# Issuing v and the DMA transposes one step ahead in a fused attention and MLP kernel

## The chip, the cores and the metric

One core of one Trainium2 chip. Times are microseconds of device time for one execution. A "span" is what the profile covers, from the first to the last instruction of one execution; a run takes about 2 us more than its span. Ratios are the mean time of one kernel's fast runs over that of the kernel before in the same rounds, so not quite the ratio of the medians that are quoted beside them.

## The reference

Causal attention over 8 batches of 8 heads, 576 positions, 64 channels, with a bias from cumulative sums of `s`, and then a two-layer MLP on the 4608 tokens:

```python
s_pos = np.maximum(s, 0.0)
cum = np.cumsum(s_pos, axis=-1)
bias = -(cum[:, :, :, None] - cum[:, :, None, :])
scores = np.where(causal, -1000000000.0, scores + np.minimum(bias, 0.0))
attn = softmax(scores)                 # cut: written out in the reference
x = (attn @ v).transpose(0, 2, 1, 3).reshape(B * S, H * D)
h = x @ w_in                           # 512 -> 2048
out = gelu(h) @ w_out                  # 2048 -> 512
```

## The kernel before

The order of instructions on each engine is the order of the program. A step `c` of the main loop runs the MLP on 512 tokens (`l1_item` is the first layer, `l2_item` the second) and, in between, the attention of the next batch `nb = c + 1`. Heads go in four pairs. There are nine steps. The first seven carry a batch, and the last two are MLP only and are called the tail here. "Start" is what comes before the first layer of step 0.

The data of a batch comes in three ways. Casting DMAs (`cast_rows`, issued by GpSimd) copy q and k to bf16 in DRAM, transposing DMAs (`transpose_rows`, on the SP queue) bring them into `qkT`, and `load_v` (SP queue) brings v. The bias is folded into weights, so v is scaled by `wb` on VectorE (`scale_v`). GpSimd sums the squares of v, which feed a check that decides whether a slow general path must run (`square_v`). P are the exponentials of the scores, `xT` is the output of the attention and the input of the MLP, and `o_sb` is the copy of a second-layer result that is then stored. In the views PE is TensorE, PEld its weight loads, DVE VectorE, ACT ScalarE, POOL GpSimd and SPq the SP queue.

```python
for c in range(NCH):
    nb = c + 1
    l1_item(c, 0, 0, KO - 1)           # ... first layer, items 0 and 1
    if nb < B:
        scale_v(nb, STS, nc.vector)    # VectorE: five tensor_tensor of 128x512
    if nb + 1 < B:
        cast_rows(nb + 1)              # GpSimd queue: 8 casting DMAs
    for f2 in range(2, FT // 2):
        l1_item(c, f2)
    if nb < B:
        exp_set()
        l2_item(c, 0, 0, 4)
        sc_item(nb, 0)                 # scores, exp on ACT, masks on VectorE
        l2_item(c, 0, 4)
        absmax(nb, 0)
        square_v(nb)                   # GpSimd: ten tensor_tensor of 128x512 f32
        for p in range(1, NP):
            sc_item(nb, p)
            av_item(nb, p - 1)         # 28 output matmuls; needs P masked, v scaled
            l2_item(c, p, 0, 12)
            absmax(nb, p)
            # ...
        if nb + 1 < B:
            transpose_rows(nb + 1)     # SP queue: 8 transposing DMAs
            load_v(nb + 1, [nc.sync])  # SP queue: 5 loads, behind them
```

Of the kernel before, what the change touches and what calls it, by code (L numbers as in the profile page):

```python
# [19 lines left out]
def kernel(  # L20
# [10 lines left out]
    nc = tc.nc  # L31
    fp32 = mybir.dt.float32
    bf16 = mybir.dt.bfloat16
# [5 lines left out]
    B, H, S, D = q.shape  # L39
    scale = 1.0 / (D ** 0.5)  # L40
    BH = B * H
    ST = 5
    NR = 6
    PR = S // NR
    SL = S - 512
    NP = H // 2
# [17 lines left out]
    PW = sum(UW)  # L64
# [51 lines left out]
    w_in_r = const.tile([128, KO, dff], bf16, name="w_in_r")  # L116
    w_out_r = const.tile([128, FT, KO * 128], bf16, name="w_out_r")
    vv = [const.tile([128, ST, H, D], bf16, name=f"vv{i}") for i in range(2)]
    qk_bf = const.tile([PR, 2, NR, H, D], bf16, name="qk_bf")
    qkT = [const.tile([128, 2, NP, 640], bf16, name=f"qkT{i}") for i in range(2)]  # L120
    for t in vv:
        nc.gpsimd.memset(t[64:128, ST - 1, :, :], 0.0)
# [8 lines left out]
    def load_qk(n, p):  # L131
        src = q if n == "q" else k
        if p == 0:
            raws[0, n] = work.tile([PR, H, NR, D], fp32, tag=f"raw{n}", bufs=1, name=f"raw_{n}")
        nc.sync.dma_start(
            out=raws[0, n][:, 2 * p : 2 * p + 2].rearrange("p h r d -> p h (r d)"),
            in_=bass.AP(
                tensor=src.tensor,
                offset=src.offset + 2 * p * S * D,
                ap=[[NR * D, PR], [S * D, 2], [1, NR * D]],  # L140
            ),
        )

    def cast(n, p, eng):
        hs = slice(2 * p, 2 * p + 2)
        i = 0 if n == "q" else 1
        eng.tensor_copy(
            qk_bf[:, i, :, hs].rearrange("p r h d -> p h r d"), raws[0, n][:, hs]
        )
# [55 lines left out]
    def scale_v(b, sts, eng, h0=0, h1=H):  # L205
        t = raws[b, "v"]
        vb = vv[b % 2]
        for st0, st1 in sts:
            n_st = 128 if st1 < ST else SL
            eng.tensor_tensor(  # L210
                vb[:n_st, st0:st1, h0:h1, :],
                t[:n_st, st0:st1, h0:h1, :],
                wb[:n_st, st0:st1, b * H + h0 : b * H + h1]
                .unsqueeze(3).to_broadcast([n_st, st1 - st0, h1 - h0, D]),
                op=MULT,
            )
# [3 lines left out]
    def load_w(which, i):  # L220
        if which == 0:
            src = moe_w_in.rearrange("(ko p) f -> p ko f", p=128)[:, :, i * 512 : (i + 1) * 512]
            dst = w_in_r[:, :, i * 512 : (i + 1) * 512]
        else:
            src = moe_w_out.rearrange("(fo p) m -> p fo m", p=128)[:, i * 4 : (i + 1) * 4, :]
            dst = w_out_r[:, i * 4 : (i + 1) * 4, :]
        nc.gpsimd.dma_start(out=dst, in_=src)
# [12 lines left out]
    def weights_pe():  # L240
        t_ps = ps.tile([128, ST, BH], fp32, tag="av", bufs=3, name="t_ps")
        for st in range(ST):
            n_st = 128 if st < ST - 1 else SL
            nc.tensor.transpose(
                t_ps[:n_st, st, :], cum[:, st * 128 : st * 128 + n_st], ident[:64, :64]
            )
        nc.scalar.activation(wb[:, 0 : ST - 1], t_ps[:, 0 : ST - 1], func=AF.Exp)
        nc.scalar.activation(wb[:SL, ST - 1], t_ps[:SL, ST - 1], func=AF.Exp)
# [97 lines left out]
    P_of = {}  # L346

    def sc_item(b, p):
        P_of[b, p] = P = work.tile([128, 2, PW], bf16, tag="P", bufs=2, name="P")
        for u in range(NU):  # L350
            s_ps = ps.tile([128, 2, 512], fp32, tag="sc", bufs=2, name="sc_ps")
            for jt, i0, n, off in UNITS[u]:
                for e in range(2):
                    nc.tensor.matmul(  # L354
                        s_ps[:, e, off : off + n],
                        lhsT=qkT[b % 2][e * 64 : e * 64 + 64, 1, p, jt * 128 : jt * 128 + 128],
                        rhs=qkT[b % 2][e * 64 : e * 64 + 64, 0, p, i0 : i0 + n],
                        start=True, stop=True,
                    )
            nc.scalar.activation(  # L360
                P[:, :, UO[u] : UO[u] + UW[u]], s_ps[:, :, : UW[u]], func=AF.Exp, scale=scale
            )
            d = P[:, :, UO[u] : UO[u] + 512].rearrange("p e (g c) -> p e g c", c=256)[:, :, :, 0:128]
            nc.vector.tensor_tensor(  # L364
                d, d, tri_bf.unsqueeze(1).unsqueeze(1).to_broadcast([128, 2, 2, 128]), op=MULT
            )
            if u == 1:
                d = P[:, :, UO[u] + 448 : UO[u] + 512]
                nc.vector.tensor_tensor(  # L369
                    d, d, tri_bf[:, :64].unsqueeze(1).to_broadcast([128, 2, 64]), op=MULT  # L370
                )

    def av_item(b, p):
        P = P_of[b, p]
        vb = vv[b % 2]
        todo = []
        for c, (c0, cn) in enumerate(ICH):
            o_ps = ps.tile([128, 2, 256], fp32, tag="av", bufs=3, name="av")
            for den in range(2):
                for n_part, (jt, lo, n, off) in enumerate(PARTS[c]):  # L380
                    for e in range(2):
                        nc.tensor.matmul(  # L382
                            o_ps[e * 64 : e * 64 + 64, den, lo : lo + n],
                            lhsT=(
                                wb[:, jt, b * H + 2 * p + e : b * H + 2 * p + e + 1].to_broadcast([128, 64])
                                if den
                                else vb[:, jt, 2 * p + e, :]
                            ),
                            rhs=P[:, e, off : off + n],
                            start=(n_part == 0),  # L390
                            stop=n_part == len(PARTS[c]) - 1,
                            skip_group_check=True,
                        )
            todo.append(o_ps)
        for c, (c0, cn) in enumerate(ICH):
            o_ps = todo[c]
            ln = work.tile([128, 256], fp32, tag="ln", bufs=3, name="ln")
            nc.scalar.activation(ln[:, :cn], o_ps[:, 1, :cn], func=AF.Ln, scale=math.exp(-LNC[c]))  # L398
            nc.scalar.activation(  # L399
                ln[:, :cn], ln[:, :cn], func=AF.Exp, scale=-1.0, bias=lnb[:, c : c + 1]  # L400
            )
            t0 = b * S + c0
            nc.vector.tensor_tensor(xT[:, p, t0 : t0 + cn], o_ps[:, 0, :cn], ln[:, :cn], op=MULT)  # L403
# [54 lines left out]
    for p in range(NP):  # L458
        cast("q", p, nc.gpsimd)
        cast("k", p, nc.gpsimd)  # L460

    def start_pair(p):
        tr_item(p, 0)
        tr_item(p, 1)
        sc_item(0, p)

    ALLV = [(0, ST - 1), (ST - 1, ST)]
    start_pair(0)
    weights_pe()
    start_pair(1)  # L470
    scale_v(0, ALLV, nc.vector, 0, 2)
    av_item(0, 0)
    for i in range(4):
        load_w(0, i)
    scale_v(0, ALLV, nc.gpsimd, 4, 8)
    cast_rows(1)
    for i in range(4):
        load_w(1, i)
    transpose_rows(1)
    load_v(1, [nc.sync])  # L480
    square_v(0)
    start_pair(2)
    scale_v(0, ALLV, nc.vector, 2, 4)
    av_item(0, 1)
    start_pair(3)
    av_item(0, 2)
    av_item(0, 3)
    for p in range(NP):
        absmax(0, p)

    for c in range(NCH):
        nb = c + 1
        l1_item(c, 0, 0, KO - 1)
        l1_item(c, 1, 0, KO - 1)
        l1_item(c, 0, KO - 1)
        l1_item(c, 1, KO - 1)
        if nb < B:
            scale_v(nb, STS, nc.vector)
        if nb + 1 < B:
            cast_rows(nb + 1)  # L500
        for f2 in range(2, FT // 2):
            l1_item(c, f2)
        if nb < B:
            exp_set()
            l2_item(c, 0, 0, 4)
            sc_item(nb, 0)
            l2_item(c, 0, 4)
            absmax(nb, 0)
            square_v(nb)
            for p in range(1, NP):  # L510
                sc_item(nb, p)
                av_item(nb, p - 1)
                l2_item(c, p, 0, 12)
                absmax(nb, p)
                if p == NP - 1:
                    av_item(nb, p)
                l2_item(c, p, 12)
            if nb + 1 < B:
                transpose_rows(nb + 1)
                load_v(nb + 1, [nc.sync])  # L520
            if c == 0:
                cert_decay()
        else:
            for sub in range(4):
                l2_item(c, sub)
                if c == B - 1:
                    (cert_1, cert_2, cert_3, cert_4)[sub]()
# [150 lines left out]
```

## Time and profile before

The median is 425.02 us (four runs, 422.63 to 431.89), the span of the profiled run 420.4. I cut the span into steps at the first matmul of each first layer in the TensorE timeline:

| | start | step 0 | steps 1 to 5, mean | step 6 | tail |
|---|---|---|---|---|---|
| before | 39.1 | 49.2 | 43.8 | 43.7 | 69.3 |

The page of the profile: busy time of TensorE, and in 40 slices of 10.5 us the granted clock of TensorE in tenths.

```profile
PE 335.9 (80%) x2426; PEld 171.6 (41%) x2426; DVE 208.7 (50%) x353; ACT 224.2 (53%) x356; POOL 206.6 (49%) x169
...
PEclk9999995999889997999699989996999799999999
```

TensorE is 80% busy, and the clock falls to half again and again, once in most steps. The waits of TensorE (what it waited for, us in total, how often, the longest):

```profile
PE av L382 <- DVE P L364: 40.5, 14, 10.7
PE o_ps L437 <- DVE o_sb L444: 7.8, 15, 1.2
```

The great wait is that of the output matmuls (`av`) for VectorE's mask of P. One step shows it, in the TensorE timeline (start, us, what, how many; in brackets the idle time before and who ended it):

```profile
132.05 3.62 PE L420 MATMUL h_ps<-xT,w_in_r 128*128 128x512 bf16 x16
...
151.07 0.62 PE L354 MATMUL sc_ps<-qkT_101 64*128 64x256 bf16 x10
157.02 0.53 PE L382 MATMUL av<-P,vv_98 128*64 128x256 bf16 x4 [5.33 <-DVE P L364]
...
158.43 0.64 PE L382 MATMUL av<-P,vv_98 128*64 128x256 bf16 x6 [0.55 <-DVE P L364]
...
160.01 5.29 PE L437 MATMUL o_ps<-w_out_r,gT 128*128 128x512 bf16 x16 [0.23 <-DVE o_sb L444]
```

TensorE has nothing to do from 151.7 to 157.0. The timeline of VectorE says why the mask is late:

```profile
148.60 0.69 DVE L210 TENSOR_TENSOR vv_98<-raw_v,wb 128x512 bf16<-128x512 f32 x1 [14.80 <-DMA raw_v<-in_v_dram]
...
151.58 0.82 DVE L210 TENSOR_TENSOR vv_98<-raw_v,wb 128x512 bf16<-128x512 f32 x1 [0.85 <-DMA raw_v<-in_v_dram]
154.37 2.27 DVE L210 TENSOR_TENSOR vv_98<-raw_v,wb 128x512 bf16<-128x512 f32 x2 [1.96 <-DMA raw_v<-in_v_dram]
156.56 1.81 DVE L364 TENSOR_TENSOR P<-P,tri_bf 128x512 bf16<-128x512 bf16 x2
158.30 1.05 DVE L369 TENSOR_TENSOR P<-P,tri_bf 128x128 bf16<-128x128 bf16 x1
```

VectorE's queue is in order. The five scalings of v stand in front of the masks and wait for v, which arrives piece by piece from 148.6 us on, the fourth of five pieces at 154.4, so 16 to 22 us into the step that began at 132.05. v is late because of its place on the SP queue: eight transposes, 1.2 us of issue each, are ahead of it.

```profile
134.70 1.16 SPq L167 DMA_TRANSPOSE qkT_101<-rows_0_0_1025  x1
...
143.79 1.22 SPq L167 DMA_TRANSPOSE qkT_101<-rows_1_3_1039  x1
145.10 2.17 SPq L173 DMA_DIRECT2D raw_v<-in_v_dram  x3
```

After the idle time TensorE is slow. These are stretches of the same step, each with its length, the busy time of the engines (PE, PEld, DVE, ACT, POOL, each with the number of its instructions), the granted clock, the DMA share (it adds up the times of packets and goes above 1 in some views) and GB/s:

```profile
157.00:160.00 3.00, 2.20 (x28) 1.98 (x28) 3.00 (x4) 1.33 (x4) 2.92 (x3) 0.50 0.00 0
160.00:165.30 5.30, 5.29 (x18) 1.92 (x19) 5.30 (x8) 0.91 (x3) 5.22 (x6) 0.68 0.13 50
```

The clock is 0.50 for 3 us and 0.68 for the next 5. The Trainium skill ("TensorE: Matmul & The Clock Gate", What's actually happening) says that the clock gate halves TensorE's clock after an idle window of about 3.4 us, that the window runs freely, and that a busy one brings full speed back. The trace agrees with the halving: 0.50 after 5.3 us of idle time.

### The profile page before, as it was taken

How to read it: one execution, taken by the hardware profiler on the slowest of the kernel's cores; microseconds unless marked ns; L12 is line 12 of the kernel's file. 1: busy time of each engine (PE TensorE's matmuls, PEld its weight loads, DVE VectorE, ACT ScalarE, POOL GpSimd, SP SyncE). 2: the span in 40 equal slices, each digit the busy share in tenths (PEclk: the TensorE clock that was granted, in tenths of full speed). 3: DMA queues.
4: the chain of work that ended last, by engine and by line, in shares of the span. 5: the costliest groups of instructions: out<-in, count | busy, mean ns of one | idle time of the engine just before them, and what ended most of it. 6: DMA issues, size and time to landing. Idle time of an engine off the chain costs nothing.

```text
span 420.4 us, 6347 instructions
## 1 busy us (share of the span) xinstructions
PE 335.9 (80%) x2426; PEld 171.6 (41%) x2426; DVE 208.7 (50%) x353; ACT 224.2 (53%) x356; POOL 206.6 (49%) x169
## 2 busy tenths in 40 slices
PE   2447953999499949996899868995999599988983
PEld 1335422544345424543454335443544354433431
DVE  4446316760985059705971397229831984023011
ACT  1447662586548554856286727773667457501500
POOL 8889999900993089505980499039001920000000
PEclk9999995999889997999699989996999799999999
DMA  8999998966389454956097809880127201011011
GB/s 202 211 189 172 183 175 83 128 105 148 48 97 132 112 101 52 138 123 128 25 151 110 154 26 132 117 167 27 50 76 152 51 27 51 0 51 51 1 51 55
DMA packets 148150, 42.58 MB, mean 101 GB/s; under 512 B 137808, under 2 KB 143441, under 8 KB 148113
## 3 DMA queue, kind: packets, MB, share of 16 engines
q0 software_dynamic: 69632, 12.46, 37.1%
q1 hardware_dynamic: 78480, 29.65, 31.5%
q8 instruction: 21, 0.34, 0.3%
q14 instruction: 17, 0.13, 0.1%
HBM read 36.85 MB, written 17.69 MB: 130 GB/s over the span
## 4 chain that ended last, share of the span: by engine, by line
PE 48%; DVE 16%; DMA 14%; SPq 14%; issue 4%; ACT 2%; POOL 1%; DVEq 0%; ACTq 0%; POOLq 0%
PE o_ps L437 24%; PE h_ps L420 18%; DMA raw_v<-in_v_dram 11%; SPq L167 8%; SPq L173 5%; PE av L382 4%; DVE P L364 4%; DVE vv_97 L210 3%; DVE P L369 3%; DVE vv_98 L210 2%; DVE o_sb L444 2%; ACT gT L426 2%; DMA rows_1_0_278<-in_k_dram 2%; PE sc_ps L354 1%; DVE amx L184 1%
## 5 line engine op out<-in xcount | busy, mean ns | idle before, releaser
L437 PE MATMUL o_ps<-w_out_r,gT 128*128 128x512 bf16 x576 | 142.8, 400 | 8.4 <-DVE o_sb L444 7.8
L420 PE MATMUL h_ps<-xT,w_in_r 128*128 128x512 bf16 x576 | 127.2, 379 | 6.2 <-ACT gT L426 6.2
L194 POOL TENSOR_TENSOR sq<-raw_v 128x512 f32<-128x512 f32 (+1 forms) x40 | 57.4, 1435 | 124.0 <-DMA raw_v<-in_v_dram 124.0
L426 ACT ACTIVATE gT<-h_ps 128x1024 bf16<-128x1024 f32 x63 | 63.5, 1022 | 60.5 <-PE h_ps L420 60.5
L360 ACT ACTIVATE P<-sc_ps 128x1024 bf16<-128x1024 f32 x64 | 62.0, 1021 | 60.3 <-PE sc_ps L354 55.4
L437 PEld LDWEIGHTS <-gT 128*128 128x128 bf16 x576 | 56.7, 102 | 78.2 <-issue 23.1
L420 PEld LDWEIGHTS <-w_in_r 128*128 128x128 bf16 x576 | 56.2, 98 | 75.2 <-issue 8.7
L195 POOL TENSOR_TENSOR sumv<-sumv,sq 128x512 f32<-128x512 f32 (+1 forms) x40 | 57.2, 1430 | 3.1
L210 DVE TENSOR_TENSOR vv_98<-raw_v,wb 128x512 bf16<-128x512 f32 (+1 forms) x20 | 21.5, 1092 | 67.4 <-DMA raw_v<-in_v_dram 67.4
L398 ACT ACTIVATE ln<-av 128x256 f32<-128x256 f32 (+1 forms) x96 | 30.7, 320 | 43.2 <-PE av L382 42.9
L444 DVE COPY o_sb<-o_ps 128x512 f32<-128x512 f32 x36 | 24.5, 681 | 53.7 <-PE o_ps L437 53.6
L364 DVE TENSOR_TENSOR P<-P,tri_bf 128x512 bf16<-128x512 bf16 x64 | 41.1, 660 | 18.0 <-ACT P L360 17.8
L399 ACT ACTIVATE ln<-ln,lnb 128x256 f32<-128x256 f32 (+1 forms) x96 | 43.6, 454 | 3.1
L210 DVE TENSOR_TENSOR vv_97<-raw_v,wb 128x512 bf16<-128x512 f32 (+2 forms) x19 | 21.9, 1188 | 46.5 <-DMA raw_v<-in_v_dram 46.4
L403 DVE TENSOR_TENSOR xT<-av,ln 128x256 bf16<-128x256 f32 (+1 forms) x96 | 32.6, 352 | 15.4 <-ACT ln L399 13.8
L382 PE MATMUL av<-P,vv_98 128*64 128x128 bf16 (+2 forms) x224 | 18.2, 250 | 26.5 <-DVE P L364 26.3
L382 PE MATMUL av<-P,vv_97 128*64 128x128 bf16 (+2 forms) x224 | 19.3, 263 | 23.4 <-DVE P L364 14.2
L382 PE MATMUL av<-P,wb 128*64 128x128 bf16 (+2 forms) x448 | 33.7, 256 | 0.0
L382 PEld LDWEIGHTS <-vv_98 128*64 128x64 bf16 x224 | 12.2, 119 | 30.3 <-issue 28.4
L382 PEld LDWEIGHTS <-vv_97 128*64 128x64 bf16 x224 | 12.7, 127 | 27.6 <-issue 18.2
L382 PEld LDWEIGHTS <-wb 128*64 128x64 bf16 x448 | 23.7, 128 | 0.2
L184 DVE TENSOR_REDUCE amx<-qkT_101 128x2 f32<-128x1152 bf16 x16 | 21.4, 1337 | 0.0
(131 smaller groups left out, 345.1 us busy)
## 6 DMA issues: line engine op xcount, KB each, us to landing
out_dram<-o_sb SPq DMA_DIRECT2D x36, 256.0 KB, 2.1
raw_v<-in_v_dram SPq DMA_DIRECT2D x32, 256.0 KB, 4.9
w_in_r<-in_moe_w_in_dram POOLq DMA_DIRECT2D x4, 512.0 KB, 9.1
w_out_r<-in_moe_w_out_dram POOLq DMA_DIRECT2D x4, 512.0 KB, 14.9
raw_q<-in_q_dram SPq DMA_DIRECT2D x4, 288.0 KB, 6.0
raw_k<-in_k_dram SPq DMA_DIRECT2D x4, 288.0 KB, 6.7
raw_v<-in_v_dram SPq DMA_DIRECT2D x8, 128.0 KB, 4.7
s_sw<-in_s_dram SPq DMA_DIRECT2D x1, 144.0 KB, 3.0
```

Source lines behind the costliest of these rows:

```text
L167: nc.sync.dma_start_transpose(out=qkT[b % 2][:, i, p, :S], in_=rows_of.pop((b, i, p)))
L194: nc.gpsimd.tensor_tensor(sq[:n_st], t[:n_st, st], t[:n_st, st], op=MULT)
L195: nc.gpsimd.tensor_tensor(sumv[:n_st], sumv[:n_st], sq[:n_st], op=ALU.add)
L210: eng.tensor_tensor(vb[:n_st, st0:st1, h0:h1, :], t[:n_st, st0:st1, h0:h1, :], wb[:n_st, st0:st1, b * H + h0 : b * H + h1] .unsqueeze(3).t ...
L360: nc.scalar.activation(P[:, :, UO[u] : UO[u] + UW[u]], s_ps[:, :, : UW[u]], func=AF.Exp, scale=scale)
L364: nc.vector.tensor_tensor(d, d, tri_bf.unsqueeze(1).unsqueeze(1).to_broadcast([128, 2, 2, 128]), op=MULT)
L382: nc.tensor.matmul(o_ps[e * 64 : e * 64 + 64, den, lo : lo + n], lhsT=(wb[:, jt, b * H + 2 * p + e : b * H + 2 * p + e + 1].to_broadcast([ ...
L399: nc.scalar.activation(ln[:, :cn], ln[:, :cn], func=AF.Exp, scale=-1.0, bias=lnb[:, c : c + 1])
L420: nc.tensor.matmul(h_ps[:, i, :], lhsT=w_in_r[:, ko, ft * 128 : (ft + 1) * 128], rhs=xT[:, ko, c * NB : (c + 1) * NB], start=(ko == 0), st ...
L426: nc.scalar.activation(gT_of[c][:, f2 * 2 : f2 * 2 + 2, :], h_ps, func=AF.Gelu)
L437: nc.tensor.matmul(o_ps, lhsT=gT[:, ft, sub * 128 : (sub + 1) * 128], rhs=w_out_r[:, ft, :], start=(ft == 0), stop=(ft == FT - 1),)
L444: nc.vector.tensor_copy(o_sb, o_ps)
```

## The change

The intent: v and the transposes of batch `nb + 1` are issued at the start of step `c` instead of at its end, so that they are there a whole step before use. The casts go two steps ahead. The squares stand before the casts, right after the scaling. For the first batch the scores of all pairs come first, then the outputs of all pairs, which needs four P buffers. `qk_bf` shares its memory with `gT` to pay for them.

```diff
@@ -346,7 +347,7 @@
-        P_of[b, p] = P = work.tile([128, 2, PW], bf16, tag="P", bufs=2, name="P")
+        P_of[b, p] = P = work.tile([128, 2, PW], bf16, tag="P", bufs=4, name="P")
     # cut: qk_bf moves from the constant pool to tag "gT" of the work pool
@@ -458,46 +459,45 @@  (start)
-    start_pair(0)        # cut: pairs 0 and 1, av_item(0, 0), w_in, cast_rows(1),
-    ...                  # w_out, transpose_rows(1), load_v(1), square_v(0),
-    av_item(0, 3)        # pairs 2 and 3 with their outputs
+    for i in range(4):
+        load_w(0, i)
+    cast_rows(1)
+    for i in range(4):
+        load_w(1, i)
+    cast_rows(2)
+    square_v(0)
+    load_v(1, [nc.sync])
+    transpose_rows(1)
+    for p in range(NP):
+        tr_item(p, 0)
+        tr_item(p, 1)
+        sc_item(0, p)
+        # cut: weights_pe and scale_v of batch 0
+    for p in range(NP):
+        av_item(0, p)
     for c in range(NCH):
         nb = c + 1
+        if nb + 1 < B:
+            transpose_rows(nb + 1)
+            load_v(nb + 1, [nc.sync])
         # cut: l1_item 0 and 1
         if nb < B:
             scale_v(nb, STS, nc.vector)
-        if nb + 1 < B:
-            cast_rows(nb + 1)
+            square_v(nb)
+        if nb + 2 < B:
+            cast_rows(nb + 2)
         # cut
             absmax(nb, 0)
-            square_v(nb)
         # cut
-            if nb + 1 < B:
-                transpose_rows(nb + 1)
-                load_v(nb + 1, [nc.sync])
```

More of the change, by code (lines that the diff above doesn't have):

```diff
@@ L118 @@
     vv = [const.tile([128, ST, H, D], bf16, name=f"vv{i}") for i in range(2)]
-    qk_bf = const.tile([PR, 2, NR, H, D], bf16, name="qk_bf")
     qkT = [const.tile([128, 2, NP, 640], bf16, name=f"qkT{i}") for i in range(2)]
@@ L142, in load_qk @@
         )
+    qk_bf = work.tile([PR, 2, NR, H, D], bf16, tag="gT", bufs=1, name="qk_bf")
     def cast(n, p, eng):
@@ L460 @@
         cast("k", p, nc.gpsimd)
-    def start_pair(p):
+    for i in range(4):
[7 more added lines that the diff above has]
+    transpose_rows(1)
+    ALLV = [(0, ST - 1), (ST - 1, ST)]
+    for p in range(NP):
         tr_item(p, 0)
@@ L465, in start_pair @@
         sc_item(0, p)
-    ALLV = [(0, ST - 1), (ST - 1, ST)]
-    start_pair(0)
-    weights_pe()
-    start_pair(1)
-    scale_v(0, ALLV, nc.vector, 0, 2)
-    av_item(0, 0)
-    for i in range(4):
-        load_w(0, i)
-    scale_v(0, ALLV, nc.gpsimd, 4, 8)
-    cast_rows(1)
-    for i in range(4):
-        load_w(1, i)
-    transpose_rows(1)
-    load_v(1, [nc.sync])
-    square_v(0)
-    start_pair(2)
-    scale_v(0, ALLV, nc.vector, 2, 4)
-    av_item(0, 1)
-    start_pair(3)
-    av_item(0, 2)
-    av_item(0, 3)
+        if p == 0:
+            weights_pe()
+        if p == 2:
+            scale_v(0, ALLV, nc.vector, 0, 4)
+    scale_v(0, ALLV, nc.vector, 4, 8)
+    for p in range(NP):
+        av_item(0, p)
     for p in range(NP):
```

## The prediction

> **What bounds the kernel now.** In the chain of waits TensorE holds 48%, VectorE 16%, DMA and the SP queue 14% each. By the TensorE timeline the span of 420.4 us is 39.1 us of start, 49.3 for step 0, six steps of 43.2 to 44.5, and two MLP-only tails, 69.3 together. In each attention step TensorE does its first layer and two score blocks, then idles 3.6 to 5.3 us (10.7 in step 0) before the first output matmul. The waits view puts 40.5 us of this down to VectorE's mask of P, 7.5 to its scaling of v. The mask is late because the scaling before it waits for v: the chain reads eight transposes of 1.2 us on the SP queue, the v load, the scaling. After the idle time the granted clock is 0.50 for 3 us and 0.7 for 5: 28 output matmuls take 2.8 us instead of 1.0, 16 second-layer matmuls 5.3 instead of 3.6. The Trainium skill ("TensorE: Matmul & The Clock Gate", What's actually happening) says that an idle window of 3.4 us halves the clock; the trace agrees.
>
> **What changes.** v and its transposes arrive a step before use, so the scaling runs during the first layer, where VectorE idles. No work is removed. Off the critical path per step: 3.6 to 5.3 us of idle time and 3.5 us of slow clock. Undisturbed, a step is 14.7 us (first layer, 0.7 of it waiting for GELU) plus 20.9 (the rest): 35.6 us.
>
> **What is given back.** GpSimd's squares of v (14 to 16 us a batch) wait for the v load, which still follows eight transposes (10 us) and lands 15 us into a step. They then run, for the batch after next, beside the masks as now. Under them a mask takes 1.1 us instead of 0.42, the small one 1.2 instead of 0.2; a VectorE block is then 6.1 us against TensorE's 5.1. I expect 3 us of short waits per step, too short to lower the clock: 38.7 us for steps 1 to 5, 36 for step 6 (no squares left), 40 for step 0, where DMA is full until 65 us.
>
> Start: scores take about 5.3 us a pair, then four outputs 3.3 us each, bound by PSUM buffers and the ACT and VectorE finish: 38.5 us, almost no gain. Tails unchanged.
>
> Sum: 38.5 + 40 + 5 x 38.7 + 36 + 69.3 = 377 us of span. The profiled run took 1.8 us more than its span, the timed median 5.8; I add 2. Predicted **379 us**, 367 to 392 in 8 of 10. Chances: faster by over 2% 0.97, within 2% 0.02, slower 0.01.
>
> **What would show it right.** The scaling no longer waits for v; TensorE's wait for the mask falls from 40 us to under 12; granted clock near 1.0 from step 1 on, mean over 0.97; TensorE busy near 312 us, since slow matmuls vanish; steps of 38 to 39 us with masks averaging 0.6 us or more, step 6 shorter by 2 to 3.
>
> **What would make it wrong.** The squares may fall in the first layer: steps of 36 us, time about 363. Or DMA, with casts, transposes and loads of three batches at once (share 0.75 in a 44 us step, 0.9 in 37), is the new limit: late transposes, outputs queued behind them, steps of 41 us. In the start, early loads and casts could delay weights or the first transposes past 54 us.

## The result and the profile after

The median is 380.75 us (four runs, 377.8 to 382.42), against 425.02 of before. The ratio is 0.897, 95% interval 0.888 to 0.906. Executions over 1.5% slower than the fastest of the same kernel are left out of the means. The profiled span is 380.0 us.

| | start | step 0 | steps 1 to 5, mean | step 6 | tail | span |
|---|---|---|---|---|---|---|
| before | 39.1 | 49.2 | 43.8 | 43.7 | 69.3 | 420.4 |
| predicted | 38.5 | 40 | 38.7 | 36 | 69.3 | 377 |
| after | 36.7 | 44.1 | 38.7 | 35.4 | 70.1 | 380.0 |

The page, as before (line numbers are one higher than in the kernel before), and the waits of TensorE:

```profile
PE 321.6 (85%) x2426; PEld 164.6 (43%) x2426; DVE 200.2 (53%) x353; ACT 222.6 (59%) x356; POOL 188.5 (50%) x167
...
PEclk9999899999999999999999999999999999999998
```

```profile
PE o_ps L438 <- DVE o_sb L445: 13.3, 16, 1.2
...
PE av L383 <- DVE xT L404: 7.5, 11, 2.1
...
PE av L383 <- DVE P L365: 2.3, 4, 0.8
PE o_ps L438 <- DMA w_out_r<-in_moe_w_out_dram: 1.7, 1, 1.7
PE av L383 <- DVE P L370: 1.4, 3, 0.5
```

The wait for the masks went from 40.5 us to 2.3 + 1.4 = 3.7, the clock is full in all of the loop from step 1 on, and in exchange the short waits grew: for o_sb from 7.8 to 13.3, for xT from 1.5 to 7.5. One of the steps 1 to 5, on TensorE, on VectorE and on GpSimd (it begins at 196.28):

```profile
196.28 3.62 PE L421 MATMUL h_ps<-xT,w_in_r 128*128 128x512 bf16 x16
...
215.29 0.62 PE L355 MATMUL sc_ps<-qkT_100 64*128 64x256 bf16 x10
215.87 0.36 PE L383 MATMUL av<-P,vv_98 128*64 128x256 bf16 x4
...
218.26 0.22 PE L383 MATMUL av<-P,vv_98 128*64 128x64 bf16 x2 [0.55 <-DVE P L370]
...
223.51 0.35 PE L383 MATMUL av<-P,vv_98 128*64 128x256 bf16 x4 [0.50 <-DVE xT L404]
...
225.83 3.61 PE L438 MATMUL o_ps<-w_out_r,gT 128*128 128x512 bf16 x16 [1.23 <-DVE o_sb L445]
```

```profile
197.94 3.08 DVE L211 TENSOR_TENSOR vv_98<-raw_v,wb 128x512 bf16<-128x512 f32 x5
214.58 2.41 DVE L365 TENSOR_TENSOR P<-P,tri_bf 128x512 bf16<-128x512 bf16 x2 [13.56 <-ACT P L361]
216.92 1.28 DVE L370 TENSOR_TENSOR P<-P,tri_bf 128x128 bf16<-128x128 bf16 x1
...
221.84 1.28 DVE L370 TENSOR_TENSOR P<-P,tri_bf 128x128 bf16<-128x128 bf16 x1
...
226.37 0.22 DVE L370 TENSOR_TENSOR P<-P,tri_bf 128x128 bf16<-128x128 bf16 x1
```

```profile
213.15 1.04 POOL L195 TENSOR_TENSOR sq<-raw_v 128x512 f32<-128x512 f32 x1 [12.16 <-DMA raw_v<-in_v_dram]
...
224.11 1.26 POOL L196 TENSOR_TENSOR sumv<-sumv,sq 64x512 f32<-64x512 f32 x1
```

The scaling is done in 3.08 us during the first layer and waits for nothing. The output matmuls start at 215.87, when the score matmuls end. But v of the batch after next lands 17 us into the step, again behind eight transposes, and starts the squares. From 213 to 225 they run beside the masks. A small mask (128x128) takes 1.28 us under them and 0.22 after them (226.37). The Trainium skill ("SBUF — State Buffer", Who interferes with whom) says that a VectorE instruction with two SBUF inputs contends with a GpSimd instruction that reads SBUF, and that a `tensor_reduce` never does. The traces agree on both: the masks and the scalings (two SBUF inputs) stretch, and the maximum (`tensor_reduce`) takes 1.33 to 1.34 us with and without squares beside it.

### The profile page after: what moved, and what is told of

Its sections match the earlier page's. It is cut to its first block, busy times and chain, and to the rows that moved or that the text cites. A ratio compares the mean times of both kernels' runs of the same rounds, so it can differ in the third digit from the quotient of the medians.

```text
span 380.0 us, 6316 instructions
## 1 busy us (share of the span) xinstructions
PE 321.6 (85%) x2426; PEld 164.6 (43%) x2426; DVE 200.2 (53%) x353; ACT 222.6 (59%) x356; POOL 188.5 (50%) x167
## 4 chain that ended last, share of the span: by engine, by line
PE 54%; DVE 13%; DMA 12%; ACT 9%; issue 6%; POOL 2%; SPq 1%; DVEq 0%; ACTq 0%
PE h_ps L421 29%; PE o_ps L438 21%; DMA rows_0_3_153<-in_q_dram 6%; DMA w_out_r<-in_moe_w_out_dram 5%; DVE P L365 4%; PE av L383 4%; ACT P L361 3%; DVE P L370 3%; DVE o_sb L445 3%; DVE amx L185 2%; ACT gT L427 2%; DMA raw_k<-in_k_dram 2%; DVE xT L404 2%; ACT L450 2%; ACT gT L430 1%
## 5 line engine op out<-in xcount | busy, mean ns | idle before, releaser
L438 PE MATMUL o_ps<-w_out_r,gT 128*128 128x512 bf16 x576 | 132.8, 379 | 15.7 <-DVE o_sb L445 13.3
L365 DVE TENSOR_TENSOR P<-P,tri_bf 128x512 bf16<-128x512 bf16 x64 | 46.6, 749 | 94.4 <-ACT P L361 94.2
L421 PEld LDWEIGHTS <-w_in_r 128*128 128x128 bf16 x576 | 56.4, 98 | 78.2 <-issue 12.6
L438 PEld LDWEIGHTS <-gT 128*128 128x128 bf16 x576 | 54.3, 97 | 77.8 <-issue 17.0
L196 POOL TENSOR_TENSOR sumv<-sumv,sq 128x512 f32<-128x512 f32 (+1 forms) x40 | 52.0, 1301 | 3.1
L400 ACT ACTIVATE ln<-ln,lnb 128x256 f32<-128x256 f32 (+1 forms) x96 | 43.6, 454 | 3.1
L383 PE MATMUL av<-P,wb 128*64 128x128 bf16 (+2 forms) x448 | 29.9, 238 | 0.0
L383 PE MATMUL av<-P,vv_97 128*64 128x128 bf16 (+2 forms) x224 | 18.1, 251 | 5.9 <-DVE xT L404 4.3
L185 DVE TENSOR_REDUCE amx<-qkT_100 128x2 f32<-128x1152 bf16 x16 | 21.5, 1341 | 0.0
L185 DVE TENSOR_REDUCE amx<-qkT_99 128x2 f32<-128x1152 bf16 x16 | 21.2, 1341 | 0.0
L355 PE MATMUL sc_ps<-qkT_99 64*128 64x256 bf16 (+2 forms) x160 | 12.0, 280 | 9.9 <-DVE qkT_99 L343 9.9
L383 PE MATMUL av<-P,vv_98 128*64 128x128 bf16 (+2 forms) x224 | 15.9, 230 | 5.3 <-DVE xT L404 3.2
L370 DVE TENSOR_TENSOR P<-P,tri_bf 128x128 bf16<-128x128 bf16 x32 | 20.3, 633 | 0.0
L383 PEld LDWEIGHTS <-vv_97 128*64 128x64 bf16 x224 | 12.3, 121 | 9.5 <-issue 8.5
```

What stands on the lines that cost most here:

```text
L185: nc.vector.tensor_reduce(amx[:, b * NP + p], qkT[b % 2][:, :, p, :S], axis=AX, op=ALU.max, apply_absolute_value=True)
L196: nc.gpsimd.tensor_tensor(sumv[:n_st], sumv[:n_st], sq[:n_st], op=ALU.add)
L365: nc.vector.tensor_tensor(d, d, tri_bf.unsqueeze(1).unsqueeze(1).to_broadcast([128, 2, 2, 128]), op=MULT)
L383: nc.tensor.matmul(o_ps[e * 64 : e * 64 + 64, den, lo : lo + n], lhsT=(wb[:, jt, b * H + 2 * p + e : b * H + 2 * p + e + 1].to_broadcast([ ...
L400: nc.scalar.activation(ln[:, :cn], ln[:, :cn], func=AF.Exp, scale=-1.0, bias=lnb[:, c : c + 1])
L421: nc.tensor.matmul(h_ps[:, i, :], lhsT=w_in_r[:, ko, ft * 128 : (ft + 1) * 128], rhs=xT[:, ko, c * NB : (c + 1) * NB], start=(ko == 0), st ...
```

## The experiments

My theory had two parts. First, the gain is that v no longer waits behind the transposes, since VectorE's queue, and TensorE with it, hung on v. Second, the 3 us that steps 1 to 5 still lose above 35.6 are the masks slowed by the squares. The rivals were that the earlier transposes and casts, or the new start, bring the gain, and that DMA traffic is what holds the steps at 38.7. Twelve kernels ran, all correct, all with three timed rounds. Three of them (x3, x10, x11) do only a fifth of the squares: the output is the same, but the check that the squares feed is weaker, so they are probes and no candidates.

All steps of all runs, in us (from the TensorE timeline of each profiled run), with the median and the ratio to the kernel before in the same rounds:

| run | start | step 0 | step 1 | steps 2 to 5, mean | step 6 | median | ratio |
|---|---|---|---|---|---|---|---|
| before | 39.1 | 49.2 | 43.7 | 43.8 | 43.7 | 425.02 | 1 |
| after | 36.7 | 44.1 | 38.8 | 38.7 | 35.4 | 380.75 | 0.897 |
| x1_v_early | 41.7 | 52.9 | 37.4 | 38.9 | 35.4 | 391.49 | 0.915 |
| x2_start_only | 37.3 | 39.0 | 48.2 | 44.1 | 44.2 | 418.74 | 0.982 |
| x3_fifth_squares | 37.0 | 41.7 | 37.2 | 35.8 | 35.4 | 364.47 | 0.852 |
| x4_warm | 40.7 | 49.4 | 43.7 | 44.6 | 44.0 | 427.30 | 1.002 |
| x5_gate | 37.4 | 44.7 | 38.1 | 35.4 | 35.4 | 368.72 | 0.867 |
| x6_v_late | 37.0 | 43.9 | 38.8 | 35.7 | 35.7 | 369.16 | 0.868 |
| x7_gate_sq0 | 37.1 | 41.3 | 38.5 | 35.4 | 35.4 | 365.16 | 0.859 |
| x8_swap | 40.2 | 37.3 | 40.5 | 35.7 | 35.6 | 368.79 | 0.868 |
| x9_start_swap | 37.1 | 40.0 | 43.0 | 35.7 | 35.7 | 370.07 | 0.864 |
| x10_before_fifth | 41.2 | 49.4 | 37.6 | 39.2 | 38.3 | 395.48 | 0.926 |
| x11_before_fifth_warm | 40.6 | 49.5 | 39.0 | 39.1 | 39.0 | 395.54 | 0.927 |
| x12_before_sq_moved | 40.6 | 43.2 | 41.6 | 43.6 | 39.8 | 410.29 | 0.965 |

### x1: only the load of v earlier

```diff
         nb = c + 1
+        if nb + 1 < B:
+            load_v(nb + 1, [nc.sync])
         l1_item(c, 0, 0, KO - 1)
 ...
                 transpose_rows(nb + 1)
-                load_v(nb + 1, [nc.sync])
```

> The kernel before, with one thing of the change: the load of v(nb+1) is issued at the start of the step instead of at its end; transposes, casts and the first batch stay. If the time comes from v no longer waiting behind the eight transposes (mine), steps 1 to 5 fall from 43.7 to about 38.7 us as in the changed kernel, step 0 keeps its 49 us (its v is still loaded late), span about 387, time about 389 us. If the earlier transposes or the casts two steps ahead are needed for the gain (rival), it stays above 410 us.

Steps 1 to 6 are those of the whole change, with casts and transposes where they were. The rest, 391.5 against 389 us, is in the start and in step 0, where the load of v of batch 2 now comes right behind that of batch 1; I did not test that part. In the main loop the load of v alone brings the gain; the earlier transposes and the second step of the casts add nothing there.

### x2: only the new start

```diff
-    cast_rows(2)          # start of the changed kernel, otherwise kept
 ...                       # main loop: that of the kernel before
```

> The changed start (scores of all pairs, then outputs; v(1) and transposes(1) issued early, no casts of batch 2 there), the loop of before. Mine: the start is worth about 2 us and the early v(1) takes the 10.7 us idle time out of step 0, so step 0 about 40 us, steps 1 to 6 unchanged at 43.7: span about 409, time about 411 us. Rival, that the start carries most of the gain: below 395 us.

The time is a miss (418.7 against 411). Start and step 0 came as expected (37.3 and 39.0), steps 2 to 6 too. Step 1 did not: 48.2 instead of 43.7 us. Its transposes are issued 2.2 us and its v 12.8 us into the step, where the kernel before has 2.2 and 12.6. What differs is GpSimd: with v early it is done with its squares, and it issues the casts of batch 3 from 2 us into the step on, beside the transposes and v. In the kernel before they come 30 us into the step.

```profile
78.42 10.51 SPq L168 DMA_TRANSPOSE qkT<-rows  x8
89.03 8.95 SPq L174 DMA_DIRECT2D raw_v<-in_v_dram  x5
```

```profile
78.49 5.38 POOL L160 DMA_DIRECT2D rows<-in_q_dram  x4
```

The five loads of v take 8.95 us to issue instead of 4.07, the first scaling starts 21.0 us into the step instead of 16.0, and TensorE waits 8.7 us for the mask. I read this as the casts of batch 3 delaying v; no run separates it. The start as such gains little: 0.982, with an interval of 0.976 to 0.989 that is too near to 2% to call.

### x3: a fifth of the squares

```diff
-        for st in range(ST):        # in square_v
+        for st in range(1):
```

> The changed kernel with only one of five row blocks squared on GpSimd (the bound that the squares feed is then weaker, the output is the same). Mine: the 3 us over 35.6 that steps 1 to 5 still lose are the masks slowed by the squares: steps about 36 us, masks near 0.45 us in mean instead of 0.75, time about 365 us. Rival, that DMA or the output stores queued behind the transposes hold the steps: steps stay above 38 us, time above 377.

The expected 365 against 364.5 measured, steps 2 to 5 at 35.8. DMA does not hold the steps: in the changed kernel steps 1 to 5 have mean DMA shares of 1.37, 1.14, 1.15, 0.81 and 0.37 and all take 37.9 to 39.2 us. Step 3 of x3 has a share of 1.32 (150 GB/s), more than step 3 of the changed kernel, and is 2.1 us shorter. The second part of the theory holds.

### x4: keeping TensorE warm in the kernel before

```diff
                 sc_item(nb, p)
+                if p == 1:
+                    warm = ps.tile([128, 512], fp32, tag="av", bufs=3, name="warm")
+                    for i in range(16):
+                        nc.tensor.matmul(
+                            warm, lhsT=w_in_r[:, 0, 0:128], rhs=w_in_r[:, 1, 0:512],
+                            start=(i == 0), stop=(i == 15),
+                        )
                 av_item(nb, p - 1)
```

> The kernel before, with 16 extra matmuls (about 3.6 us at full clock, result unused) in the idle time before the first output block of each step. Mine: the idle time stays but the clock no longer falls, so in steps 1 to 6 the output block and the 16 matmuls after it run at full clock: up to 3.5 us a step less, of which the VectorE blocks, then the longer ones, keep about 1; steps about 41.2, time about 410 us. Rival, that these matmuls are slow for another reason than the idle time: granted clock still 0.5 there, time 425 us or more.

This was a miss. The mean clock rose (0.964 to 0.978 in the four runs, 0.917 to 0.933 for the kernel before in the same rounds) and the time did not move (1.002, interval 0.996 to 1.008). But the clock did not stay up: it still fell once in each of steps 1 to 6, only later. The first output block now runs at a clock of 0.90 to 1.00. In steps 1, 3, 5 and 6 the 16 matmuls after it still take 5.0 to 5.2 us (step 1 is the first line below). In steps 2 and 4 they take 3.61 us, but the waits for VectorE around them grow, and the clock falls one block later. Step 2 (it begins at 133.88) is the rest of what is shown (x15 stands where a matmul's record is missing from the trace):

```profile
117.46 5.22 PE L437 MATMUL o_ps<-w_out_r,gT 128*128 128x512 bf16 x15 [0.32 <-DVE o_sb L444]
...
153.45 3.63 PE L515 MATMUL warm<-w_in_r 128*128 128x512 bf16 x15
157.97 0.35 PE L382 MATMUL av<-P,vv 128*64 128x256 bf16 x4 [0.89 <-DVE P L364]
...
160.96 3.61 PE L437 MATMUL o_ps<-w_out_r,gT 128*128 128x512 bf16 x16 [0.32 <-DVE o_sb L444]
...
168.18 5.30 PE L437 MATMUL o_ps<-w_out_r,gT 128*128 128x512 bf16 x15 [1.23 <-DVE o_sb L444]
```

```profile
161.00:164.60 3.60, 3.60 (x18) 1.52 (x19) 3.60 (x4) 0.28 (x1) 3.44 (x4) 1.00 0.19 73
164.60:173.40 8.80, 6.71 (x53) 3.34 (x52) 6.39 (x13) 3.96 (x8) 8.80 (x9) 0.81 1.04 93
```

VectorE is busy without a break from 154.6 to 171 us here, from the last scalings to the third block, as in the kernel before. I read this as VectorE being the longer chain, so that a faster TensorE beside it gains nothing. Step 4 of the kernel before (from 220.64 on) speaks for it: its 16 matmuls took 4.30 us, about 1 us less than in step 2, TensorE then waited 1.23 us for `o_sb`, and the step took 43.6 us like the others. The reading is argued from the traces, and x11 was meant to test it. What x4 shows is that a slow stretch that is only moved later saves nothing. It does not show what the slow clock costs in the kernel before, since the clock still fell.

### x10 and x11: a fifth of the squares in the kernel before, without and with the warm matmuls

> The kernel before with one of five row blocks squared. Mine: v still comes late, so TensorE still idles about 4 us and runs at half clock after; only VectorE's scaling and masks get shorter. Steps 42 to 43 us instead of 43.7, time about 417 us. Rival, that the squares alone explain the wait: below 395 us.

> x10 with the 16 extra matmuls of x4. With all squares the extra matmuls gained nothing; my reason is that VectorE, slowed by the squares, was the longer chain there. With VectorE relieved the slow clock should be what is left: 2.5 to 3.5 us a step less than x10 in steps 1 to 6, so about 15 to 20 us less, about 400 us. Rival, that the slow clock costs nothing here for another reason: the same time as x10.

Both were misses, and x10 the more telling. With v still late, and nothing moved, taking away four fifths of the squares brought 31 us, to 395.5. In the kernel before v's late arrival starts the scaling and the squares at the same moment. They then fight: in one step (beginning at 88.3) five scalings took 7.80 us, where they take 3.08 in the changed kernel, and the masks follow under the same squares. Late v is dear mostly through this.

In x10 the six waits of steps 1 to 6 for the first mask are 2.04, 3.60, 3.07, 2.83, 2.18 and 2.79 us. The clock fell after the second and the fourth and not after the others; these are the stretches after the second (3.60), third (3.07) and fourth (2.83):

```profile
151.40:157.60 6.20, 5.94 (x43) 2.98 (x43) 5.18 (x11) 2.13 (x6) 6.20 (x6) 0.72 1.51 131
191.60:197.00 5.40, 5.33 (x59) 3.12 (x61) 5.40 (x12) 2.46 (x7) 5.40 (x7) 1.00 1.46 134
229.90:236.00 6.10, 5.81 (x43) 3.00 (x43) 5.21 (x12) 2.13 (x6) 6.10 (x7) 0.72 1.59 138
```

A gap of 2.83 us brought the half clock and one of 3.07 did not, which fits a window that runs freely and is not reset by the gap. The two steps with the fall take 40.7 and 39.9 us, the four without 37.6 to 38.6; the fourth and the sixth have almost the same wait (2.83 and 2.79 us) and take 39.9 with the fall and 38.3 without. So here, where VectorE is not busy throughout (5.2 of the 6.2 us after the second wait), a fall costs about 1.5 us beyond its gap (40.7 - 35.6 - 3.6 = 1.5). In x11 there is no fall, and all steps are 39.0 to 39.3: the same mean, since the output block now starts a little later. In the step looked at, v lands 17.8 us into it, against 16.6 in the step of x10 that I compared. Why v came later in x11 was not tested and stays open, so x11 does not say what the clock costs, and my reading of x4 remains argued.

### x12: all the squares in the kernel before, moved

```diff
             scale_v(nb, STS, nc.vector)
+        if c < B:
+            nc.gpsimd.tensor_copy(gate, xT[:, NP - 1, nb * S - 1 : nb * S])
+            square_v(c)
         if nb + 1 < B:
             cast_rows(nb + 1)
 ...
             absmax(nb, 0)
-            square_v(nb)
```

The tiny copy reads the last column that the batch before writes into `xT`, so GpSimd can't pass it before the step begins. (`square_v(0)` is gone from the start.)

> The kernel before with all squares done, but those of batch c at the start of step c instead of those of c+1 in its second half (held there by a tiny GpSimd copy that reads the last xT column). v still arrives 16 us into its step, behind the transposes. If the place of the squares, not their amount, made the late v dear (what x10 suggests): steps as in x10, 38 to 40 us, time about 395 us. If x10 was fast only since work was missing: 415 us or more.

The time is 410.3, between the two and a miss. The scalings and masks run undisturbed now (0.69 and 0.21 us in the trace), but in steps 1 to 5 the casts came to be issued beside the load of v, from 138 us on in a step that began at 125.4, and v's five pieces landed between 142.5 and 150.7. So this edit moved two things and does not decide for those steps. Step 6 has no casts in either kernel, and there all of the squares are done in both: 39.8 us against 43.7, near the 38.3 of x10. That step speaks for the place of the squares and not their amount.

### x5 and x7: the squares held back in the changed kernel

```diff
             scale_v(nb, STS, nc.vector)
+            nc.gpsimd.tensor_copy(gate, xT[:, NP - 1, nb * S - 1 : nb * S])
             square_v(nb)
```

and for x7 also, in the start:

```diff
-    cast_rows(2)
     square_v(0)
+    cast_rows(2)
```

> The changed kernel with one tiny GpSimd copy ahead of each batch's squares, which reads the last column of the batch before in xT and so holds the squares until the step begins. Mine: squares then run beside the first layer and the scaling, not beside the masks; steps 1 to 5 about 36 us, time about 365 us, as with a fifth of the squares but with all of the work. Rival, that it was the amount of GpSimd work or of DMA and not its place: no change, 378 to 382.

> x5 with the squares of batch 0 ahead of the casts of batch 2 in the start. Mine: step 0 loses its late squares of two batches in a row[...], step 0 falls from 44 to about 41; about 2 to 3 us faster than x5, about 362 us. Rival: step 0 is held by late weights and transposes, no change against x5.

With all the work kept, and only moved to the first layer, steps 2 to 5 are 35.4 us: what TensorE needs. Squares that share the time with the scalings cost nothing, since both end before the masks begin. A step of x7:

```profile
154.01 7.51 DVE L211 TENSOR_TENSOR vv<-raw_v,wb 128x512 bf16<-128x512 f32 x5
170.65 0.42 DVE L366 TENSOR_TENSOR P<-P,tri_bf 128x512 bf16<-128x512 bf16 x1 [9.13 <-ACT P L362]
...
171.90 0.22 DVE L371 TENSOR_TENSOR P<-P,tri_bf 128x128 bf16<-128x128 bf16 x1
```

These masks take 0.42 and 0.22 us while GpSimd issues the casting DMAs (from 167.3 us in this trace). The Trainium skill ("SBUF — State Buffer", Who interferes with whom) says that a `tensor_tensor` was not seen to stall such DMAs, and infers that it takes only the read interface of the shared ports, while writing the DMA's descriptors needs the write interface. This trace shows the other direction: the masks were not held up either.

x5 missed its time by 4 us, 368.7 for 365, because step 0 (44.7) and step 1 (38.1) stayed: there GpSimd is behind. In the changed kernel its queue waits at the start for earlier DMAs to land, up to 60 us, and then has the squares of two batches to do. One of these waits, in its trace:

```profile
29.42 1.32 POOL L160 DMA_DIRECT2D rows_1_2_159<-in_k_dram  x1 [2.00 <-DMA w_in_r<-in_moe_w_in_dram]
```

x7 does the first squares before the second casts, and step 0 falls to 41.3. Its 365.2 us (362 expected) is the fastest of the complete kernels that ran.

### x6 and x8: v ahead of the transposes

x6 is the changed kernel with `load_v(nb + 1)` back at the end of the step. x8 is the kernel before with two lines swapped:

```diff
             if nb + 1 < B:
-                transpose_rows(nb + 1)
                 load_v(nb + 1, [nc.sync])
+                transpose_rows(nb + 1)
```

(and the same two calls for batch 1 in the start).

> The changed kernel with the load of v(nb+1) put back at the end of the step, as in the kernel before; the transposes stay at the start of the step. v then goes ahead of the next transposes on the SP queue. Mine: what hurt was the place of v behind the transposes, not its distance: v lands by about 7 us into its step, in time for the scaling, and the squares start 8 us earlier than now, so steps about 36.5 us, time about 367. Rival, that v must be a whole step ahead: the idle time returns, above 395 us.

> The kernel before with two lines swapped, in the loop and in the start: v(nb+1) is loaded ahead of the transposes instead of behind them; nothing is earlier by a step. Mine: v lands about 7 us into the step, the transposes from 10 to 17 us, before each pair's scores; the idle time goes and the squares fall mostly in the first layer: steps about 36.5 us, time about 370, faster than the whole change. Rival, that transposes and casts must be a step ahead too: scores wait for transposes, steps above 40, time above 395.

Both came as expected: steps 2 to 6 at 35.7. The first piece of v lands 5.5 us into the step of x8 shown here (beginning at 153.73), the transposes are issued after it, and the scaling and most of the squares fall into the first layer:

```profile
155.93 4.32 SPq L173 DMA_DIRECT2D raw_v<-in_v_dram  x5
160.35 10.67 SPq L167 DMA_TRANSPOSE qkT<-rows  x8
```

```profile
159.25 0.69 DVE L210 TENSOR_TENSOR vv<-raw_v,wb 128x512 bf16<-128x512 f32 x1 [3.77 <-DMA raw_v<-in_v_dram]
...
172.04 1.68 DVE L364 TENSOR_TENSOR P<-P,tri_bf 128x512 bf16<-128x512 bf16 x2 [5.86 <-ACT P L360]
```

So v did not have to be a step ahead; it was enough that it came ahead of the transposes. (In x1 it stays behind the transposes of an earlier batch and is a step ahead, which is enough for the idle time too, but leaves the squares beside the masks.) The swap alone, at 368.8 us, is faster than the whole change at 380.75.

### x9: the new start with the swap

> The changed start, and the loop of before with v loaded ahead of the transposes (x2 and the loop half of x8). Mine: start 37, step 0 39 as in x2, step 1 about 38, then 35.7 each as in x8: span about 362, time about 364 us, level with the best so far. Against: in x2 step 1 was 48 us since the casts of batch 2 came late; if that is not cured by the order alone, step 1 stays above 43 and the time above 368.

A miss by 6 us. Step 1 takes 43.0 us: its scores wait 5.2 us for transposes; x8 has the same wait, 3.8 us. The reason that I gave, late casts of batch 2, is not borne out: in x2 and x9 they were issued from 55 us on, and the DMA share is 0.00 in the first 2.2 us of step 1, before its transposes are issued, so they had landed. What the traces show instead is, as in x2, the casts of batch 3 beside them: in x9 they are issued from 1.3 us into the step on, and v and the transposes take 8.2 and 13.7 us to issue, against 4.3 and 10.7 in the step of x8 shown above. In the changed kernel the transposes and v that step 1 needs are issued by 84.8 us, before the casts of batch 3 (from 85.4), and step 1 has no such wait. That is what being a step ahead pays for, as far as these traces show.

## Why the prediction was right

- **The time.** 379 predicted, 380.75 measured. The sum was built from what a step needs, 35.6 us, plus what I expected to be lost, and both terms hold: undisturbed steps are 35.4 (x5) and steps 1 to 5 lost 3.1 us. x3 and x5 show that it is the squares that cost them. That the sum came so near is in part luck: the misses of step 0 (+4.1), start (-1.8), tail (+0.8) and step 6 (-0.6) partly cancel.
- **The mechanism of the gain.** Right, and the chain of cause was shown on the chip: x1 moves only v and gets the loop's whole gain.
- **"Off the critical path per step: 3.6 to 5.3 us of idle time and 3.5 us of slow clock".** The second half is not shown as a cost. x4 kept the clock up over the first output block and won nothing, and the trace has VectorE busy without a break there; but the clock still fell later in each step, so x4 puts no price on the 3.5 us. The only price is x10's, about 1.5 us a fall, in a kernel with a fifth of the squares. The total did not suffer, since the sum was not built by subtracting from the old step.
- **"Too short to lower the clock".** True of the changed kernel (1.00 in steps 1 to 6), but the shortness of single waits does not explain it: in x4 the clock fell although no single gap before the fall was longer than 1.23 us. That it stayed up is in part luck.
- **"7.5 to its scaling of v".** All three of these waits lie in the start (before 39 us), so they were no part of the idle time of the steps.
- **What I missed about the kernel before.** I took the lateness of v as the cost and the squares as a burden of the new kernel only. x10 shows that, with v still late, most of the 8 us a step goes with the squares: steps of 38.9 on average instead of 43.8. The two costs overlap: v early saves 5.1 us a step, four fifths of the squares 4.9, both together (x3) 7.8.
- **Step 0**, "40", took 44.1. The runs name two parts. The squares of batch 0 behind the casts of batch 2 are worth 3.4 us (44.7 in x5, 41.3 in x7). Without casts of batch 2 in the start and with those squares early (x2, where the step also starts no transposes and load of batch 2) it is 39.0. In the trace it also waits 1.7 us for w_out. This is partly what I had named as a risk, early casts delaying the weights. Outputs queued behind the transposes, the other risk, did occur: VectorE waited 6.5 us once for an output store. It fell into the first layer of step 1 and cost little there: in x3 the same wait was 14.1 us, and that step took 37.2 us.
- **TensorE busy "near 312 us"** was 321.6. The term was mis-sized: I counted the time of the whole slow output block, 2.8 us, as slow matmuls, but part of that was waiting (0.55 us inside the block shown above), and step 0's first layer now runs slow (its last 48 matmuls took 12.2 us, against 10.5 elsewhere). By an estimate from these figures (7 x 0.55 + 1.7) they make up about 5.5 of the 9.6 us; the rest was not traced.
- **Signs named in advance.** Wait for the mask under 12: 3.7. Mean clock over 0.97: 0.992. Mean mask of 0.6 us or more: 0.749 after (0.660 before). Step 6 shorter by 2 to 3: by 3.3. Start 38.5: 36.7.

## What to carry to other kernels

When an in-order queue makes a small load wait behind bulky ones, first try to swap them; loading a step earlier may not be needed. When an engine off the critical path slows another by working beside it, look for the moment at which its inputs release it, and tie it to a stage where the other engine is free: here one tiny copy that waits for the right thing was worth 12 us (380.75 to 368.7). And a slow clock after an idle gap is not by itself a cost to subtract: ask which chain ends last once it is gone, and check that the clock does not fall again a little later, as it did in x4.

## What the Trainium skill lacked or had wrong

- "TensorE: Matmul & The Clock Gate" warns of idle gaps over about 3.4 us (HAM oscillation), and says that frequent short idle times can also make the clock go up and down, but not how short. In x10 a gap of 2.83 us was followed by a clock of 0.72 on average over the next 6 us, while one of 3.07 us left it at 1.00, which fits the page's window that runs freely. In x4 the clock fell at 168 us with no single gap before it longer than 1.23 us; from 164.6 to 168.0 TensorE was busy for 1.61 of 3.40 us.
- The same page counts the extra time of cold matmuls as time lost to the kernel. In x4 the mean clock rose from 0.917 to 0.933 (kernel before, same rounds) to 0.964 to 0.978, and the time changed by +0.2%. In x10, where VectorE is not busy throughout, a fall did cost about 1.5 us. The page lacks that another engine's work can hide the loss.
- "SBUF — State Buffer" says that the second of two contenders blocks, but gives no size for small instructions. Here a 128x128 mask went from 0.22 to 1.28 us beside GpSimd's squares of 1.0 to 1.3 us each, and two 128x512 masks in a row took 1.93 to 2.41 us, against 0.42 for one alone: the small mask lost nearly five times its own length.
- No page that I found says at how many casting DMAs in flight GpSimd's queue stops; "Debugging Trainium Hangs" (Descriptor Overflow) names too many descriptors for the space reserved in SBUF, but as a cause of hangs. Here nothing hung. In the start of the changed kernel its queue stopped for about 2 us before single DMA issues, each time until an earlier DMA had landed.
